# Recurrence plus two-layer MLP on one core: GLA stages spread between MLP pieces, TensorE order pinned by hand

## The chip, the cores and the metric

The kernel runs on one core of a Trainium2 chip. The metric is the time of one execution in microseconds of device time, as the median of several executions. The span of a profile, from the first to the last instruction of the program, is 1.7 us shorter than the time of the same execution. The kernel is written in a framework whose scheduler, when the program is built, settles the order of every engine's instructions: unless told otherwise it may put a later instruction ahead of an earlier one when data dependencies permit and its own estimate says that this is useful. "Free" below means that, and "pinned" means that TensorE keeps the order in which the program was written.

In the lines of profiles PE is TensorE (PEld its weight loads), DVE is VectorE, ACT is ScalarE, POOL is GpSimd, SP is SyncE. L170 is line 170 of that run's kernel; in the changed kernel and its variants all matmuls go through one helper (L128 in the lines shown) and all transposes through another (L131), so that the tile's name tells them apart.

## The reference

A gated linear recurrence ("GLA") over 4 batches, 8 heads, 768 steps and head size 48, then a two-layer MLP with squared ReLU ("MoE" in the kernel, though there is no routing) over the 3072 tokens:

```python
for t in range(S):                               # S = 768, state is 48 x 48 per head
    state = alpha[:, :, t, :, None] * state + np.einsum('bhd,bhe->bhde', k[:, :, t], v[:, :, t])
    y[:, :, t] = np.einsum('bhd,bhde->bhe', q[:, :, t], state)
x = y.transpose(0, 2, 1, 3).reshape(3072, 384)
h = x @ w_in                                     # 384 -> 2048
g = np.maximum(h, 0.0) ** 2
return g @ w_out                                 # 2048 -> 384
```

## The kernel before

The tokens are cut into 24 chunks of 128. A chunk's GLA is a chain that passes between engines many times. The MoE works on groups of chunks: "MoE-1" makes `ph` (three accumulated matmuls for each of 16 slices of the hidden layer), "MoE-2" makes `po` (16 accumulated matmuls for a chunk).

```python
def gla_chunk(sc, tiles):
    nc.scalar.activation(L[:, :, 0:D], at, AF.Ln)
    nc.tensor.matmul(pm[:, 0:HD], lhsT=utri_b[:, 0, :], rhs=L[:, :, 0:D], ...)   # decay
    nc.scalar.activation(A, pm..., AF.Exp); nc.scalar.activation(Ainv, pm..., AF.Exp, scale=-1.0)
    nc.vector.tensor_mul(qA[:, :, 0:D], qt, A); nc.vector.tensor_mul(kI[:, :, 0:D], kt, Ainv)
    # 8 transposes of qA, kI on TensorE, then
    nc.vector.tensor_copy(qkT, pT)
    # 8 score matmuls, then
    nc.vector.tensor_mul(sm[:, hh], sc_ps[:, hh], utri_b...)                     # twice
    # py = q state ("inter") + sm v ("intra"), then
    nc.scalar.copy(xn, py[:, 0:HD])
    # 3 transposes of xn, then
    nc.vector.tensor_copy(xT_big[:, :, tok0:tok0 + P], pxT)
    # state update: 4 matmuls, st * ae on VectorE, sb copy on ScalarE
    ...

def moe1(g, f):
    ph = ps_h.tile([P, 512], FP32, name="ph")            # 2 buffers
    # 3 matmuls of GN[g] * 128 columns
    nc.scalar.activation(r[:, 0:n], ph[:, 0:n], AF.Relu)
    eng = nc.vector if f % 2 == 0 else nc.gpsimd
    eng.tensor_mul(gT_tiles[g][:, f, 0:n], r[:, 0:n], r[:, 0:n])

def moe2(g, tt):
    po = ps_o.tile([P, d_model], FP32, name="po")        # 1 buffer
    # 16 matmuls of 384 columns, ob = copy of po by VectorE or ScalarE, DMA out

GN = [2, 2, 4, 4, 4, 4, 2, 2]                            # chunks per MoE group
# moe_q: for each group its 16 moe1 pieces, the moe2 tiles of the group before merged in
for s in range(NT):
    ...                                                  # loads for s + 2; w_out piece for s < 4
    gla_chunk(s, pend.pop(s))
    budget = total * max(0, s - 2) / (NT - 2)
    while qi < len(moe_q) and moe_q[qi][0] <= s and spent < budget:
        ...                                              # place the next MoE piece
```

A piece can be placed only when its whole group has been through GLA, and one chunk more (`moe_q[qi][0] <= s`; chunks count from 0), and the budget grows evenly from chunk 2 on. Counting the pieces that this loop places gives, after chunks 8, 12, 16 and 20, a whole 4-chunk group at once (16 MoE-1 pieces and 2 to 4 MoE-2 tiles), and nothing after the chunks between.

## Time and profile before

| | before |
|---|---|
| time, median of 3 (237.67 to 237.98) | 237.79 us |
| span of the profile | 235.9 us |
| PE busy by the page | 194.6 us (82%) |
| TensorE's need at undisturbed spacing | 162 us (MoE 124.5, GLA 37.9) |
| DVE / ACT busy | 55% / 55% |

The third row misleads. The Trainium skill ("Perfetto Trace Analysis", Identifying the Most-Contended Engine) says that matmul busy time is a poor measure of the distance to the limit, because matmuls are pipelined. The number used here instead is the *gap*: the time from one matmul's start to the next one's start, less the spacing of such matmuls when nothing disturbs them (read from the timeline: 215.5 ns for 512 columns, 162 for 384, 109 for 256, 55.5 for 128, 42.5 for 96, 25 for 48 or 1, 28 for a 64-row score matmul). The sums of spacings and gaps below were worked out so from the trace.

The page of before: its first line of busy times, three rows of the 40 slices of 5.9 us each (tenths of busy time; PEclk is the granted clock), and the chain of work that ended last, by engine:

```profile
PE 194.6 (82%) x1696; PEld 110.0 (47%) x1696; DVE 129.2 (55%) x253; ACT 129.4 (55%) x313; POOL 68.1 (29%) x101
...
PE   0055877887989979999989899998979979999974
...
PEclk9999999999999999999999999999999999999999
DMA  7999899931999965669747664245410000011001
...
PE 57%; ACT 15%; DVE 14%; issue 6%; DMA 3%; POOL 2%; SPq 1%; ACTq 0%; DVEq 0%; POOLq 0%
```

Until 48 us (slice 8) the DMA engines are full: inputs and weights are landing. After that TensorE is never long idle and never quite full.

The waits of TensorE in before, the longest two from 0 to 50 us and then four from 50 to 192 us (total us, times, longest):

```profile
PE misc L170 <- DVE qA_s L165: 9.1, 4, 7.0
PE misc L144 <- ACT L_s L141: 4.5, 2, 4.0
...
PE misc L170 <- DVE qA_s L165: 3.5, 6, 0.6
PE sc L180 <- DVE qkT L174: 3.1, 8, 0.6
PE misc L196 <- DVE sm L184: 2.5, 7, 0.5
PE misc L203 <- ACT xn L200: 1.5, 3, 0.6
```

Each of the last four is a step of the GLA chain that waits for the step before it on another engine. Why nothing else filled these holes shows in the timeline of TensorE, 112.5 to 117 us (start, duration, operation):

```profile
112.49 1.51 PE L226 MATMUL ph<-xT_big,w_in_b 128*128 128x512 bf16 x6
113.84 0.33 PE L239 MATMUL po<-w_out_b,gT_1095 128*128 128x384 bf16 x1
114.00 1.55 PE L226 MATMUL ph<-xT_big,w_in_b 128*128 128x512 bf16 x6
115.39 0.33 PE L144 MATMUL misc<-L_s,utri_b 128*128 128x384 bf16 x1
115.62 1.49 PE L226 MATMUL ph<-xT_big,w_in_b 128*128 128x512 bf16 x6
```

Here MoE-1 runs in a burst with almost no GLA between, as the placing loop wrote it. In the stretches between bursts, GLA chains have little but MoE-2 to fill their waits: from 120 to 132 us and from 156 to 168 us the trace has not one MoE-1 matmul.

### The profile page before, as it was taken

The page shows a single profiled execution, that of the slowest core. Times are in us where ns is not written, and L with a number is a line of the kernel's source. Part 1 is how long each engine was busy: PE and PEld are TensorE (multiplying, and loading weights), DVE is VectorE, ACT ScalarE, POOL GpSimd, SP SyncE. Part 2 cuts the span into 40 slices and gives each one's busy share as a digit, 9 for nine tenths or more (in the row PEclk, how much of TensorE's full clock was granted, in tenths as well). Part 3 has the DMA queues.
Part 4 walks back from the last instruction along what each step waited for, and adds up shares of the span by engine and source line. Part 5 has one row for each costly group of instructions (what it writes and reads, how often), then busy time and mean ns, then how long its engine had stood idle before and what let it go on. Part 6 is the DMA issues. An engine that isn't in the chain of part 4 may idle for free.

```text
span 235.9 us, 4581 instructions
## 1 busy us (share of the span) xinstructions
PE 194.6 (82%) x1696; PEld 110.0 (47%) x1696; DVE 129.2 (55%) x253; ACT 129.4 (55%) x313; POOL 68.1 (29%) x101
## 2 busy tenths in 40 slices
PE   0055877887989979999989899998979979999974
PEld 0033555554544435544444554455534436655642
DVE  0257567667567376567376557375655477135320
ACT  3234777695348765538854457835467727351720
POOL 4000333442002750005630006620016623320520
PEclk9999999999999999999999999999999999999999
DMA  7999899931999965669747664245410000011001
GB/s 138 311 249 269 218 257 259 248 61 35 209 216 214 216 130 97 163 143 184 152 85 166 150 138 94 65 98 129 103 44 0 3 0 35 36 61 40 3 35 67
DMA packets 107031, 30.19 MB, mean 128 GB/s; under 512 B 100352, under 2 KB 105472, under 8 KB 107008
## 3 DMA queue, kind: packets, MB, share of 16 engines
q1 hardware_dynamic: 107008, 29.89, 54.5%
q8 instruction: 13, 0.21, 0.4%
q14 instruction: 10, 0.08, 0.1%
HBM read 25.17 MB, written 4.72 MB: 127 GB/s over the span
## 4 chain that ended last, share of the span: by engine, by line
PE 57%; ACT 15%; DVE 14%; issue 6%; DMA 3%; POOL 2%; SPq 1%; ACTq 0%; DVEq 0%; POOLq 0%
PE po L239 20%; PE ph L226 20%; ACT r L231 5%; DVE sm L184 4%; DVE qA_s L165 3%; ACT A L153 3%; PE sc L180 3%; PE misc L203 3%; PE misc L170 3%; DMA win_f<-in_moe_w_in_dram 3%; DVE qkT L174 3%; PE misc L172 2%; PE misc L196 2%; PE misc L144 2%; DVE ob L245 2%
## 5 line engine op out<-in xcount | busy, mean ns | idle before, releaser
L226 PE MATMUL ph<-xT_big,w_in_b 128*128 128x512 bf16 (+1 forms) x384 | 79.6, 328 | 1.5 <-ACT r L231 0.5
L231 ACT ACTIVATE r<-ph 128x256 bf16<-128x256 f32 (+1 forms) x128 | 61.5, 492 | 24.0 <-PE ph L226 16.6
L226 PEld LDWEIGHTS <-w_in_b 128*128 128x128 bf16 x384 | 35.5, 98 | 25.6 <-issue 8.1
L162 POOL CAST vb<-vt 128x384 bf16<-128x384 f32 x24 | 13.0, 542 | 77.0 <-DMA vt<-in_v_dram 31.4
L184 DVE TENSOR_TENSOR sm<-sc,utri_b 128x512 bf16<-128x512 f32 x48 | 30.9, 685 | 2.8 <-PE sc L180 2.4
L200 ACT CAST xn<-misc 128x384 bf16<-128x384 f32 x24 | 11.5, 479 | 25.6 <-PE misc L196 25.6
L165 DVE TENSOR_TENSOR qA_s<-qt,A 128x384 bf16<-128x384 f32 x24 | 15.8, 659 | 13.6 <-ACT A L153 13.6
L174 DVE COPY qkT<-misc 128x1024 bf16<-128x1024 bf16 x24 | 16.5, 689 | 9.9 <-PE misc L172 9.9
L170 PE MATMUL misc<-ident_bf,qA_s 128*128 128x128 bf16 x96 | 10.1, 232 | 12.9 <-DVE qA_s L165 12.6
L215 ACT CAST sb<-st 128x384 bf16<-128x384 f32 x20 | 9.6, 480 | 20.1 <-DVE st L213 19.8
L204 DVE COPY xT_big<-misc 128x384 bf16<-128x384 bf16 x24 | 8.6, 357 | 20.2 <-PE misc L203 19.9
L196 PE MATMUL misc<-vb,sm 128*128 128x48 bf16 x192 | 13.1, 188 | 7.0 <-DVE sm L184 7.0
L153 ACT ACTIVATE A<-misc 128x384 bf16<-128x384 f32 x24 | 11.8, 490 | 11.7 <-PE misc L147 11.7
L196 PEld LDWEIGHTS <-sm 128*128 128x128 bf16 x192 | 9.4, 97 | 16.6 <-DVE sm L184 15.4
L170 PEld LDWEIGHTS <-qA_s 128*128 128x128 bf16 x96 | 5.9, 101 | 21.2 <-DVE qA_s L165 14.0
L239 PE MATMUL po<-w_out_b,gT_1095 128*128 128x384 bf16 x64 | 13.8, 325 | 0.8 <-DVE ob L245 0.5
L239 PE MATMUL po<-w_out_b,gT_1538 128*128 128x384 bf16 x64 | 13.5, 325 | 0.5 <-DVE ob L245 0.2
L141 ACT ACTIVATE L_s<-at 128x384 bf16<-128x384 f32 x24 | 12.6, 523 | 2.4 <-DMA at<-in_alpha_dram 2.0
L180 PE MATMUL sc<-qkT 64*128 64x128 bf16 x192 | 10.0, 226 | 4.0 <-DVE qkT L174 4.0
L166 DVE TENSOR_TENSOR kI_s<-kt,Ainv 128x384 bf16<-128x384 f32 x24 | 13.2, 550 | 0.0
L247 ACT COPY ob<-po 128x384 f32<-128x384 f32 x12 | 5.7, 478 | 13.1 <-PE po L239 12.9
L239 PE MATMUL po<-w_out_b,gT_2031 128*128 128x384 bf16 x64 | 12.8, 325 | 0.1
(66 smaller groups left out, 290.2 us busy)
## 6 DMA issues: line engine op xcount, KB each, us to landing
at<-in_alpha_dram SPq DMA_DIRECT2D x24, 192.0 KB, 3.6
qt<-in_q_dram SPq DMA_DIRECT2D x24, 192.0 KB, 3.5
kt<-in_k_dram SPq DMA_DIRECT2D x24, 192.0 KB, 3.7
vt<-in_v_dram SPq DMA_DIRECT2D x24, 192.0 KB, 3.7
out_dram<-ob SPq DMA_DIRECT2D x24, 192.0 KB, 1.9
win_f<-in_moe_w_in_dram SPq DMA_DIRECT2D x4, 768.0 KB, 6.1
wout_f<-in_moe_w_out_dram SPq DMA_DIRECT2D x4, 768.0 KB, 5.6
```

What stands on the lines that cost most here:

```text
L153: nc.scalar.activation(A, pm[:, 0:HD].rearrange("p (h d) -> p h d", h=H), AF.Exp)
L162: nc.gpsimd.tensor_copy(vb, vt)
L165: nc.vector.tensor_mul(qA[:, :, 0:D], qt, A)
L166: nc.vector.tensor_mul(kI[:, :, 0:D], kt, Ainv)
L170: nc.tensor.transpose(pT[:, p, :], qA[:, 2 * p:2 * p + 2, :], ident_bf)
L174: nc.vector.tensor_copy(qkT, pT)
L180: nc.tensor.matmul(sc_ps[:, hh, p, :], lhsT=qkT[sl, NP + p, :], rhs=qkT[sl, p, :], start=True, stop=True)
L184: nc.vector.tensor_mul(sm[:, hh], sc_ps[:, hh], utri_b.to_broadcast([P, NP, P]))
L196: nc.tensor.matmul(py[:, h * D:(h + 1) * D], lhsT=sm[:, hh, p, :], rhs=vb[:, h, :], start=(c == 0 and h == 0), stop=True, skip_group_check ...
L226: nc.tensor.matmul(ph[:, 0:n], lhsT=w_in_b[:, j, f * P:(f + 1) * P], rhs=xT_big[:, j, t0:t0 + n], start=(j == 0), stop=(j == KT - 1),)
L231: nc.scalar.activation(r[:, 0:n], ph[:, 0:n], AF.Relu)
L239: nc.tensor.matmul(po, lhsT=gT[:, kf, tt * P:(tt + 1) * P], rhs=w_out_b[:, kf, :], start=(kf == 0), stop=(kf == FT - 1),)
```

## The change

Its intent: cut GLA into five stages and write them into the program with MoE pieces between, so that every copy on VectorE or ScalarE passes behind MoE matmuls; pin TensorE to exactly that order. Groups become 3 chunks; MoE-2 tiles are placed in quarters, alternating with MoE-1; inputs are loaded three chunks ahead instead of two; the next chunk's decay is issued before this chunk's `intra`; and the MoE of a group is spread evenly until the next group is complete. The diff holds smaller changes too: two pieces of `w_out` are now loaded before the inputs of chunk 3 (one in before), `intra` takes its heads in another order, and in the last group every second MoE-2 tile gets another PSUM buffer. The core of the diff (stage bodies are the old lines moved, cut here):

```diff
+    def mm(*a, **kw):
+        tc.keep_in_program_order(nc.tensor.matmul(*a, **kw))
+    def tr(*a):
+        tc.keep_in_program_order(nc.tensor.transpose(*a))
-    def gla_chunk(sc, tiles):
+    def st_decay(s): ...
+    def st_transpose(s): ...
+    def st_scores(s): ...        # scores, inter product and state update
+    def st_intra(s): ...
+    def st_xT(s): ...
-    def moe2(g, tt):
+    NQ = 4
+    def moe2(g, tt, qd):
+        for kf in range(qd * FT // NQ, (qd + 1) * FT // NQ): ...
-    GN = [2, 2, 4, 4, 4, 4, 2, 2]
+    GN = [1, 2, 3, 3, 3, 3, 3, 3, 3]
+    def budget(tau):
+        b = 0.0
+        for g in range(len(GN)):
+            lo, hi = ends[g], ends[g + 1]
+            b += seg_cost[g] * min(1.0, max(0.0, (tau - lo) / (hi - lo)))
+        return b
-        gla_chunk(s, pend.pop(s))
-        budget = total * max(0, s - 2) / (NT - 2)
+        seq = [lambda: st_transpose(s), lambda: st_scores(s),
+               lambda: st_decay(s + 1) if s + 1 < NT else None,
+               lambda: st_intra(s), lambda: st_xT(s)]
+        for k, f in enumerate(seq):
+            f()
+            if k == 4:
+                prog["x"] = s + 1
+            moe_until(budget(s + (k + 1) / 5))
```

More of the change, by code (lines that the diff above doesn't have):

```diff
@@ L94 @@
     nc.vector.memset(ae_s, 0.0)
-    xT = [big.tile([P, KT, P], BF16, name=f"xT{i}") for i in range(NT)] if False else None
     xT_big = big.tile([P, KT, n_tok], BF16)
@@ L125, in load_chunk, with st_decay @@
             tiles.append(t)
-        return tiles
-    state = {}
-    def gla_chunk(sc, tiles):
-        b, c = divmod(sc, NCH)
-        at, qt, kt, vt = tiles
-        tok0 = sc * P
-        i = sc % NBUF
-        if c == 0:
-            state["ps"] = ps_st.tile([P, NP, 2 * D], FP32, name="st")
-            state["b"] = None
-        st = state["ps"]
+        ch[sc] = {"in": tiles}
+    def mm(*a, **kw):
+        tc.keep_in_program_order(nc.tensor.matmul(*a, **kw))
+    def tr(*a):
+        tc.keep_in_program_order(nc.tensor.transpose(*a))
+    ch = {}
+    state = {}
+    def st_decay(s):
+        d = ch[s]
+        at, qt, kt, vt = d["in"]
+        i = s % NBUF
         L = L_s[:, i]
         nc.scalar.activation(L[:, :, 0:D], at, AF.Ln)
+        vb = work.tile([P, H, D], BF16, name="vb", bufs=3)
+        nc.gpsimd.tensor_copy(vb, vt)
+        d["vb"] = vb
         pm = ps_misc.tile([P, 512], FP32, name="misc")
-        nc.tensor.matmul(pm[:, 0:HD], lhsT=utri_b[:, 0, :], rhs=L[:, :, 0:D],
-                         start=True, stop=True)
+        mm(pm[:, 0:HD], lhsT=utri_b[:, 0, :], rhs=L[:, :, 0:D], start=True, stop=True)
         for p in range(NP):
-            nc.tensor.matmul(
-                pm[:, HD + p:HD + p + 1],
-                lhsT=L[:, 2 * p:2 * p + 2, :], rhs=ones_col,
-                start=True, stop=True,
-            )
+            mm(pm[:, HD + p:HD + p + 1], lhsT=L[:, 2 * p:2 * p + 2, :], rhs=ones_col,
+               start=True, stop=True)
+        pm3 = pm[:, 0:HD].rearrange("p (h d) -> p h d", h=H)
         A = work.tile([P, H, D], BF16, name="A")
-        nc.scalar.activation(A, pm[:, 0:HD].rearrange("p (h d) -> p h d", h=H), AF.Exp)
+        nc.scalar.activation(A, pm3, AF.Exp)
         Ainv = work.tile([P, H, D], BF16, name="Ainv")
-        nc.scalar.activation(Ainv, pm[:, 0:HD].rearrange("p (h d) -> p h d", h=H),
-                             AF.Exp, scale=-1.0)
+        nc.scalar.activation(Ainv, pm3, AF.Exp, scale=-1.0)
         ae = ae_s[:, i]
@@ L159, in gla_chunk, with st_transpose, st_scores @@
         nc.scalar.activation(ae[64:128, :, 1], pm[64:128, HD:HD + NP], AF.Exp)
-        vb = work.tile([P, H, D], BF16, name="vb")
-        nc.gpsimd.tensor_copy(vb, vt)
-        qA = qA_s[:, i]
-        kI = kI_s[:, i]
-        nc.vector.tensor_mul(qA[:, :, 0:D], qt, A)
-        nc.vector.tensor_mul(kI[:, :, 0:D], kt, Ainv)
+        nc.vector.tensor_mul(qA_s[:, i, :, 0:D], qt, A)
+        nc.vector.tensor_mul(kI_s[:, i, :, 0:D], kt, Ainv)
+    def st_transpose(s):
+        d = ch[s]
+        i = s % NBUF
+        qA, kI = qA_s[:, i], kI_s[:, i]
         pT = ps_misc.tile([P, 2 * NP, P], BF16, name="misc")
         for p in range(NP):
-            nc.tensor.transpose(pT[:, p, :], qA[:, 2 * p:2 * p + 2, :], ident_bf)
+            tr(pT[:, p, :], qA[:, 2 * p:2 * p + 2, :], ident_bf)
         for p in range(NP):
-            nc.tensor.transpose(pT[:, NP + p, :], kI[:, 2 * p:2 * p + 2, :], ident_bf)
+            tr(pT[:, NP + p, :], kI[:, 2 * p:2 * p + 2, :], ident_bf)
         qkT = work.tile([P, 2 * NP, P], BF16, name="qkT")
         nc.vector.tensor_copy(qkT, pT)
+        d["qkT"] = qkT
+    def st_scores(s):
+        d = ch[s]
+        b, c = divmod(s, NCH)
+        i = s % NBUF
+        qkT = d["qkT"]
         sc_ps = ps_sc.tile([P, 2, NP, P], FP32, name="sc")
@@ L179, in gla_chunk @@
                 sl = slice(64 * hh, 64 * hh + 64)
-                nc.tensor.matmul(sc_ps[:, hh, p, :], lhsT=qkT[sl, NP + p, :],
-                                 rhs=qkT[sl, p, :], start=True, stop=True)
+                mm(sc_ps[:, hh, p, :], lhsT=qkT[sl, NP + p, :], rhs=qkT[sl, p, :],
+                   start=True, stop=True)
         sm = work.tile([P, 2, NP, P], BF16, name="sm")
         for hh in range(2):
-            nc.vector.tensor_mul(sm[:, hh], sc_ps[:, hh],
-                                 utri_b.to_broadcast([P, NP, P]))
+            nc.vector.tensor_mul(sm[:, hh], sc_ps[:, hh], utri_b.to_broadcast([P, NP, P]))
@@ L187, in gla_chunk @@
+        d["sm"] = sm
         py = ps_misc.tile([P, 512], FP32, name="misc")
-        for p in range(NP):
-            if c > 0:
-                nc.tensor.matmul(py[:, 2 * p * D:2 * (p + 1) * D], lhsT=qkT[:, p, :],
-                                 rhs=state["b"][:, p, :], start=(p == 0), stop=False,
-                                 skip_group_check=True)
-        for p in range(NP):
-            for hh in range(2):
-                h = 2 * p + hh
-                nc.tensor.matmul(py[:, h * D:(h + 1) * D], lhsT=sm[:, hh, p, :],
-                                 rhs=vb[:, h, :], start=(c == 0 and h == 0), stop=True,
-                                 skip_group_check=True)
@@ L199, in gla_chunk @@
-        xn = work.tile([P, HD], BF16, name="xn")
-        nc.scalar.copy(xn, py[:, 0:HD])
-        pxT = ps_misc.tile([P, KT, P], BF16, name="misc")
-        for j in range(KT):
-            nc.tensor.transpose(pxT[:, j, :], xn[:, j * P:(j + 1) * P], ident_bf)
-        nc.vector.tensor_copy(xT_big[:, :, tok0:tok0 + P], pxT)
+        d["py"] = py
+        if c > 0:
+            for p in range(NP):
+                mm(py[:, 2 * p * D:2 * (p + 1) * D], lhsT=qkT[:, p, :],
+                   rhs=state["b"][:, p, :], start=(p == 0), stop=False,
+                   skip_group_check=True)
@@ L206, in gla_chunk @@
         if c < NCH - 1:
+            if c == 0:
+                state["ps"] = ps_st.tile([P, NP, 2 * D], FP32, name="st")
+            st = state["ps"]
             for p in range(NP):
-                nc.tensor.matmul(st[:, p, :], lhsT=kI[:, 2 * p:2 * p + 2, :],
-                                 rhs=vb[:, 2 * p:2 * p + 2, :],
-                                 start=(c == 0 and p == 0), stop=True,
-                                 skip_group_check=True)
+                mm(st[:, p, :], lhsT=kI_s[:, i, 2 * p:2 * p + 2, :],
+                   rhs=d["vb"][:, 2 * p:2 * p + 2, :],
+                   start=(c == 0 and p == 0), stop=True, skip_group_check=True)
@@ L212, in gla_chunk @@
             st4 = st.rearrange("p n (j e) -> p n j e", j=2)
-            nc.vector.tensor_mul(st4, st4, bcast(ae, D))
+            nc.vector.tensor_mul(st4, st4, bcast(ae_s[:, i], D))
             sb = work.tile([P, NP, 2 * D], BF16, name="sb")
@@ L216, in gla_chunk, with st_intra, st_xT @@
             state["b"] = sb
+    def st_intra(s):
+        d = ch[s]
+        c = s % NCH
+        py, sm, vb = d["py"], d["sm"], d["vb"]
+        for hh in range(2):
+            for p in range(NP):
+                h = 2 * p + hh
+                mm(py[:, h * D:(h + 1) * D], lhsT=sm[:, hh, p, :], rhs=vb[:, h, :],
+                   start=(c == 0 and h == 0), stop=True, skip_group_check=True)
+        xn = work.tile([P, HD], BF16, name="xn")
+        nc.scalar.copy(xn, py[:, 0:HD])
+        d["xn"] = xn
+    def st_xT(s):
+        xn = ch[s]["xn"]
+        pxT = ps_misc.tile([P, KT, P], BF16, name="misc")
+        for j in range(KT):
+            tr(pxT[:, j, :], xn[:, j * P:(j + 1) * P], ident_bf)
+        nc.vector.tensor_copy(xT_big[:, :, s * P:(s + 1) * P], pxT)
+        del ch[s]
     gT_tiles = {}
+    po_cur = {}
     def moe1(g, f):
@@ L225, in moe1 @@
         for j in range(KT):
-            nc.tensor.matmul(
-                ph[:, 0:n], lhsT=w_in_b[:, j, f * P:(f + 1) * P],
-                rhs=xT_big[:, j, t0:t0 + n], start=(j == 0), stop=(j == KT - 1),
-            )
+            mm(ph[:, 0:n], lhsT=w_in_b[:, j, f * P:(f + 1) * P],
+               rhs=xT_big[:, j, t0:t0 + n], start=(j == 0), stop=(j == KT - 1))
         r = rpool.tile([P, 512], BF16, name="r")
@@ L233, in moe1 @@
         eng.tensor_mul(gT_tiles[g][:, f, 0:n], r[:, 0:n], r[:, 0:n])
-    def moe2(g, tt):
-        po = ps_o.tile([P, d_model], FP32, name="po")
-        gT = gT_tiles[g]
-        for kf in range(FT):
-            nc.tensor.matmul(
-                po, lhsT=gT[:, kf, tt * P:(tt + 1) * P], rhs=w_out_b[:, kf, :],
-                start=(kf == 0), stop=(kf == FT - 1),
-            )
-        ob = opool.tile([P, d_model], FP32, name="ob")
-        if tt % 2 == 0:
-            nc.vector.tensor_copy(ob, po)
-        else:
-            nc.scalar.copy(ob, po)
-        nc.sync.dma_start(out=out_r[GT[g] + tt], in_=ob)
@@ L250 @@
-    GN = [2, 2, 4, 4, 4, 4, 2, 2]
+    NQ = 4
+    def moe2(g, tt, qd):
+        if qd == 0:
+            last = g == len(GN) - 1
+            if last and tt % 2 == 1:
+                po_cur[0] = ps_misc.tile([P, 512], FP32, name="misc")[:, 0:d_model]
+            else:
+                po_cur[0] = ps_o.tile([P, d_model], FP32, name="po")
+        po = po_cur[0]
+        gT = gT_tiles[g]
+        for kf in range(qd * FT // NQ, (qd + 1) * FT // NQ):
+            mm(po, lhsT=gT[:, kf, tt * P:(tt + 1) * P], rhs=w_out_b[:, kf, :],
+               start=(kf == 0), stop=(kf == FT - 1))
+        if qd == NQ - 1:
+            ob = opool.tile([P, d_model], FP32, name="ob")
+            if tt % 2 == 0:
+                nc.vector.tensor_copy(ob, po)
+            else:
+                nc.scalar.copy(ob, po)
+            nc.sync.dma_start(out=out_r[GT[g] + tt], in_=ob)
@@ L251 @@
+    GN = [1, 2, 3, 3, 3, 3, 3, 3, 3]
     assert sum(GN) == NT
     GT = [sum(GN[:i]) for i in range(len(GN))]
-    LEAD = 2
-    pend = {}
-    for s in range(2):
-        pend[s] = load_chunk(s)
-        if s == 0:
-            for pc in range(2):
-                load_w_in(pc, 4)
-        else:
-            for pc in range(2, 4):
-                load_w_in(pc, 4)
-    moe_q = []
-    for g in range(len(GN)):
-        done = GT[g] + GN[g]
-        items = []
-        for f in range(FT):
-            items.append((done, "1", g, f))
-        if g > 0:
-            tts = GN[g - 1]
-            step = FT // tts
-            merged = []
-            for f in range(FT):
-                merged.append(items[f])
-                if (f + 1) % step == 0:
-                    merged.append((done, "2", g - 1, (f + 1) // step - 1))
-            items = merged
-        moe_q += items
@@ L281 @@
-    for tt in range(GN[-1]):
-        moe_q.append((NT, "2", len(GN) - 1, tt))
-    def cost(it):
-        return GN[it[2]] * 3 * P if it[1] == "1" else FT * d_model
-    total = sum(cost(it) for it in moe_q)
-    qi = 0
-    spent = 0
-    for s in range(NT):
-        if s + 2 < NT:
-            pend[s + 2] = load_chunk(s + 2)
-        if s < 4:
-            load_w_out(s, 4)
-        gla_chunk(s, pend.pop(s))
-        budget = total * max(0, s - 2) / (NT - 2)
-        while qi < len(moe_q) and moe_q[qi][0] <= s and spent < budget:
-            it = moe_q[qi]
-            (moe1 if it[1] == "1" else moe2)(it[2], it[3])
-            spent += cost(it)
-            qi += 1
@@ L302 @@
-    while qi < len(moe_q):
-        it = moe_q[qi]
-        (moe1 if it[1] == "1" else moe2)(it[2], it[3])
-        qi += 1
+    segs = []
+    for g in range(len(GN) + 1):
+        ones = [("1", g, f) for f in range(FT)] if g < len(GN) else []
+        twos = [("2", g - 1, tt, qd) for tt in range(GN[g - 1]) for qd in range(NQ)] if g else []
+        n1, n2 = len(ones), len(twos)
+        i1 = i2 = 0
+        seg = []
+        while i1 < n1 or i2 < n2:
+            if i1 < n1 and (i2 >= n2 or i1 * n2 <= i2 * n1):
+                seg.append(ones[i1])
+                i1 += 1
+            else:
+                seg.append(twos[i2])
+                i2 += 1
+        segs.append(seg)
@@ new lines, with cost @@
+    items = sum(segs, [])
+    def cost(it):
+        return GN[it[1]] * 3 * P if it[0] == "1" else FT * d_model // NQ
+    total = sum(cost(it) for it in items)
+    seg_cost = [sum(cost(it) for it in seg) for seg in segs]
+    ends = [GT[g] + GN[g] for g in range(len(GN))] + [NT + 1]
+    def budget(tau):
[4 more added lines that the diff above has]
+        return b
+    prog = {"i": 0, "spent": 0, "x": 0}
@@ new lines, in moe_until @@
+    def moe_until(budget):
+        while prog["i"] < len(items) and prog["spent"] < budget:
+            it = items[prog["i"]]
+            if it[0] == "1" and GT[it[1]] + GN[it[1]] > prog["x"]:
+                return
+            if it[0] == "1":
+                moe1(*it[1:])
+            else:
+                moe2(*it[1:])
+            prog["spent"] += cost(it)
+            prog["i"] += 1
+    for s in range(2):
+        load_chunk(s)
+        for pc in range(2 * s, 2 * s + 2):
+            load_w_in(pc, 4)
@@ new lines @@
+    load_chunk(2)
+    load_w_out(0, 4)
+    load_w_out(1, 4)
+    st_decay(0)
+    for s in range(NT):
+        if s + 3 < NT:
+            load_chunk(s + 3)
+        if s < 2:
+            load_w_out(s + 2, 4)
+        seq = [lambda: st_transpose(s), lambda: st_scores(s),
[6 more added lines that the diff above has]
+            moe_until(budget(s + (k + 1) / 5))
@@ L309 @@
+    moe_until(total + 1)
 _INS = ['q', 'k', 'v', 'alpha', 'moe_w_in', 'moe_w_out']
```

## The prediction

> **What bounds the kernel now.** TensorE, but through its order rather than its work. The page shows PE 82% busy, yet that counts pipelined ends. In the timeline, undisturbed matmuls start 162 ns apart for 384 columns, 215 for 512, 109 for 256, 55 for a 128-column transpose. The Trainium skill ("TensorE: Matmul & The Clock Gate", Part 1) gives N / 2.4 GHz + 2.5 ns; 384 columns make 162.5, so the trace agrees. Summed over all matmuls (my estimate from these spacings) MoE needs 124.5 us and GLA 37.9 us: 162 us of a 236 us span. The granted clock is full throughout.
>
> Where the other 74 us are: up to 24 us PE does only 3 us of work, because inputs and weights are still landing (DMA about 250 GB/s and saturated until 48 us, page part 2). From 24 to 48 us PE does 15 us. From 48 to 228 us it loses about 39 us: the wait view names qA_s, qkT, sm, xn (VectorE and ScalarE results that the next GLA step needs) and the copy of the single po buffer; in the timeline MoE-1 runs in bursts without GLA (72-84, 108-120, 144-156, 180-190 us), then GLA chunks follow each other with only MoE-2 to fill, and each waits for its own chain. GLA steps also cost 0.1-0.13 us at each entry (scores, state product) even without a wait.
>
> **What the change does.** It adds and removes almost no work. The same products are made; the middle groups go from 512 to 384 columns (same cycles per token), so ScalarE's relu has 128 instances again, about 0.49 us each (the 384-column evictions of before) instead of 0.38/0.60: +4 us on an engine that is 55% busy. It moves: MoE is paced so that about 1 us of it stands between any two dependent GLA steps, and next chunk's decay is issued two steps early. Latencies to cover: qkT copy 0.69 us, sm 1.37, xn 0.48, A/Ainv then qA/kI about 2 us. One fifth of a chunk's MoE is 5.2/5 = 1.04 us, so scores and intra are just covered when VectorE is free, and not when a gT product (0.4), st (0.56) or ob (0.55) stands ahead; ScalarE and VectorE take their queues in order. po stays single: each of 24 tiles still waits 0.2-0.6 us beyond the one MoE-1 piece set between.
>
> **Sum.** Start: still DMA bound; six chunks and all weights by about 49 us, PE work done 20 us against 18 before: gain about 1 us. The rest, 143 us, cost 39 us of gaps before. Now (estimate): entries 0.4 us a chunk, 7; po 6; GLA waits 0.6 us a chunk, 10; together about 23 us. The last 23 us are pure MoE at nearly full rate. 49 + 143 + 23 + 3 (last copy and store) = 218; with luck in the queues 208. All of it lies on the critical path, as PE is the path. I predict **216 us**, range **206 to 229**; faster by over 2%: 0.86, within: 0.10, slower: 0.04.
>
> **Would show it right:** PE's work in 12 us windows rises from 8-10 us to 10.5 or more after 60 us, evenly, no MoE-1 bursts; PE share of the chain of waits rises above 65%; waits of PE on qA_s and qkT shrink; the first 48 us unchanged; GLA's last chunk ends about 190 us instead of 217. **Wrong:** PE waiting in order for sm, qkT or ob in every chunk, VectorE over 75% busy in the middle.
>
> **What would spoil it:** fixed order makes any late VectorE or ScalarE result stop all of TensorE, where before ready work was placed there; a chunk that waits for DMA in the first 48 us stops MoE too; the pacing leaves 23 us of MoE after the last chunk, and little MoE in the first 40 us.

## More of the kernel before

In the first 40 us some gap is only the half clock. (The clock row of the page does not show all of that: before 24 us it reads full in before, while 128-column transposes start 107 ns apart.)

## The result, and the profile after

| | before | after |
|---|---|---|
| time, median of 4 | 237.73 us | 225.14 us (224.74 to 227.79) |
| span of the profile | 235.9 us | 223.2 us |
| TensorE's need | 162.4 us | 162.5 us |
| of it done by 50 us | 19.1 us | 15.7 us |
| gaps from 50 to 192 us | 30.9 us | 20.1 us |
| gaps after 192 us | 8.2 us | 2.1 us |
| start of the last chunk's xT copy | 216.8 us | 194.4 us |

The ratio is 0.9495, with a 95% interval of 0.9421 to 0.9569: faster by 5%. Every ratio in this document is the mean time of one kernel's fast runs over that of the other's of the same rounds, so it is not quite the ratio of the medians that are quoted.

The page after:

```profile
PE 184.1 (83%) x1744; PEld 117.6 (53%) x1744; DVE 129.9 (58%) x265; ACT 125.4 (56%) x325; POOL 70.9 (32%) x109
...
PE   1057659668998898999889989999989999999994
...
PEclk9999656999999999999999999999999999999999
DMA  6999999999895384989689853543100010010011
...
PE 50%; ACT 27%; DVE 10%; issue 7%; DMA 3%; SPq 1%; ACTq 0%; DVEq 0%
```

The middle is even now, but the fifth to ninth slices together hold less TensorE work than in before, and the granted clock sinks to about half in the fifth to seventh. The last line is the chain that ended last, by engine: PE holds 50% of it (57% before), and ACT 27% (15% before).

Waits of TensorE after, from 0 to 50 us:

```profile
PE misc L128 <- ACT L_s L141: 11.3, 5, 4.3
PE misc L131 <- DVE qA_s L158: 7.1, 1, 7.1
PE ph L128 <- ACT r L243: 2.4, 3, 1.1
```

And from 50 to 192 us:

```profile
PE misc L131 <- ACT xn L220: 4.8, 8, 1.1
PE ph L128 <- ACT r L243: 2.5, 11, 0.2
PE po L128 <- DVE ob L264: 2.0, 5, 0.5
PE ph L128 <- DVE xT_big L228: 0.8, 3, 0.3
PE sc L128 <- DVE qkT L171: 0.3, 1, 0.3
```

In the middle the waits for `qA_s`, `qkT` and `sm` are all but gone (9.1 us in before, 0.3 now), while those for `xn` grew from 1.5 to 4.8 us. In the start, the wait for `L_s` is new in size: 11.3 us against 4.5 us in before. `L_s` is the first ScalarE step of a chunk, the logarithm, and needs that chunk's `alpha` to have landed. The trace shows what it holds up: between 30.4 and 33.0 us TensorE stands still for `L_s` of chunk 3, and right after it come MoE-1 pieces, `intra` and x transposes of earlier chunks. The `alpha` itself came later: those of chunks 3, 4 and 5 landed at 31.8, 38.5 and 44.9 us, against 27.6, 34.5 and 40.7 us in before. The new place of the `w_out` loads ahead of chunk 3 fits that, but no run puts them back. It is not enough for the long wait by itself: in free_groups4 below, with landings at 31.9, 38.2 and 44.8 us, the wait for `L_s` is 6.0 us.

### The profile page after: what moved, and what is told of

The parts are those of the page before. It is cut to its first block, busy times and chain, and to the rows that moved or that the text cites. A ratio compares the mean times of both kernels' runs of the same rounds, so it can differ in the third digit from the quotient of the medians.

```text
span 223.2 us, 4722 instructions
## 1 busy us (share of the span) xinstructions
PE 184.1 (83%) x1744; PEld 117.6 (53%) x1744; DVE 129.9 (58%) x265; ACT 125.4 (56%) x325; POOL 70.9 (32%) x109
## 4 chain that ended last, share of the span: by engine, by line
PE 50%; ACT 27%; DVE 10%; issue 7%; DMA 3%; SPq 1%; ACTq 0%; DVEq 0%
PE po L128 19%; PE ph L128 14%; ACT r L243 8%; PE misc L128 6%; PE misc L131 6%; ACT A L152 4%; PE sc L128 4%; ACT Ainv L154 4%; ACT xn L220 3%; DVE qkT L171 3%; DMA win_f<-in_moe_w_in_dram 3%; DVE ob L264 3%; ACT L_s L141 2%; ACT sb L207 2%; PE st L128 2%
## 5 line engine op out<-in xcount | busy, mean ns | idle before, releaser
L243 ACT ACTIVATE r<-ph 128x384 bf16<-128x384 f32 (+2 forms) x144 | 64.3, 458 | 59.5 <-PE ph L128 55.6
L128 PE MATMUL ph<-xT_big,w_in_b 128*128 128x384 bf16 (+2 forms) x432 | 85.9, 318 | 6.2 <-ACT r L243 5.0
L128 PEld LDWEIGHTS <-w_in_b 128*128 128x128 bf16 x432 | 38.2, 102 | 23.3 <-issue 6.9
L128 PE MATMUL misc<-L_s,utri_b 128*128 128x384 bf16 x24 | 8.3, 346 | 11.3 <-ACT L_s L141 11.3
L128 PEld LDWEIGHTS <-qkT 64*128 64x128 bf16 (+1 forms) x272 | 9.9, 99 | 12.2 <-DVE qkT L171 6.4
L264 DVE COPY ob<-po 128x384 f32<-128x384 f32 x16 | 8.8, 548 | 8.1 <-PE po L128 8.1
L131 PE MATMUL misc<-ident_bf,xn 128*128 128x128 bf16 x72 | 8.6, 232 | 5.7 <-ACT xn L220 5.5
L128 PEld LDWEIGHTS <-L_s 128*128 128x128 bf16 x96 | 6.1, 99 | 12.5 <-issue 10.0
L154 ACT ACTIVATE Ainv<-misc 128x384 bf16<-128x384 f32 x24 | 11.9, 496 | 0.0
L245 POOL TENSOR_TENSOR gT_2836<-r 128x384 bf16<-128x384 bf16 x8 | 6.6, 827 | 15.9 <-ACT r L243 15.9
```

Source lines behind the costliest of these rows:

```text
L128: tc.keep_in_program_order(nc.tensor.matmul(*a, **kw))
L131: tc.keep_in_program_order(nc.tensor.transpose(*a))
L154: nc.scalar.activation(Ainv, pm3, AF.Exp, scale=-1.0)
L264: nc.vector.tensor_copy(ob, po)
```

## The experiments

The first theory (A) was the change's own: the hand-made order on TensorE brings the gain. The rival (B): the gain comes from what was rewritten in the program, and pinning it adds nothing. The second question was the start, which cost more than I had predicted. Twelve kernels ran, all correct.

| run | order | difference | time us | ratio to before |
|---|---|---|---|---|
| after | pinned | | 225.14 | 0.9495 |
| free_order | free | none else | 218.33 | 0.9182 |
| before_fixed | pinned | before's program | 338.26 | 1.4241 |
| whole_moe2 | pinned | whole MoE-2 tiles | 236.48 | 0.9942 |
| free_whole | free | whole MoE-2 tiles | 220.02 | 0.9246 |
| groups_of_4 | pinned | old groups | 222.05 | 0.9344 |
| free_groups4 | free | old groups | 211.34 | 0.8894 |
| start_late | pinned | decay late in first six chunks | 228.14 | 0.9587 |
| warm | pinned | extra matmuls in the start | 225.79 | 0.9494 |
| before_quarters | free | before + quarter tiles | 236.85 | 0.9951 |
| before_paced | free | before + even pacing | 224.37 | 0.9443 |
| free_block | free | MoE after each whole chunk | 216.95 | 0.9142 |
| best | free | groups 1,1,2,2,3,3,4,4,2,2 | 217.31 | 0.9154 |

### Is it the pinned order?

**free_order** takes the pinning away and leaves everything else.

```diff
     def mm(*a, **kw):
-        tc.keep_in_program_order(nc.tensor.matmul(*a, **kw))
+        nc.tensor.matmul(*a, **kw)
     def tr(*a):
-        tc.keep_in_program_order(nc.tensor.transpose(*a))
+        nc.tensor.transpose(*a)
```

> The changed kernel without the pinning of TensorE's order: stages, 3-chunk groups, quarter tiles and the program's order stay, but the scheduler may move matmuls as it did before. Theory A (the gain comes from the order fixed by hand on TensorE): about 232 to 238 us, gaps between matmuls from 48 us on back near 36 us, MoE-1 bursts again. Rival B (the gain comes from the new program order, pacing and pieces, which the scheduler would follow anyway): 223 to 227 us, as the changed kernel's 225.1.

It ran in 218.33 us (ratio 0.9182, 0.9156 to 0.9207). Both theories had missed the direction: pinned, the same program takes about 3% longer (0.9495 / 0.9182 = 1.034, each against before in its own rounds). Theory A falls. The scheduler did reorder: about half of TensorE's matmuls stand at another place in the list, and the lists of VectorE and ScalarE shift with it, so this is not a test of TensorE's order alone. Waits of TensorE in free_order, three from 0 to 50 us and one from 50 to 192 us:

```profile
PE misc L131 <- DVE qA_s L158: 8.3, 3, 6.8
PE misc L128 <- ACT L_s L141: 4.2, 1, 4.2
PE misc L128 <- DVE sm L187: 2.2, 6, 0.6
...
PE misc L131 <- ACT xn L220: 1.3, 3, 0.9
```

The wait for `L_s` is back at before's size. By 50 us TensorE has done 17.8 us of its work (15.7 pinned). In the middle the wait for `xn` is 1.3 us (4.8 pinned).

**before_fixed** is the kernel before with all matmuls and transposes through `mm` and `tr`, pinned.

> The kernel before with nothing but TensorE pinned to program order. Its program has a whole GLA chunk without MoE in it, then the MoE pieces. Theory A says that the order is what matters, so an unspread order must be bad when pinned: each chunk's chain (about 6 us in the first chunks of before, of which TensorE works 1.6 us) stands open, 24 times about 4 us: 290 us or more. Rival B (pinning itself helps): at or under 238 us.

338.26 us. The expectation of a far longer time holds; it says only that a program whose GLA chunk is one block relies on the scheduler for its overlap. The mean granted clock was 0.798, so the halts also cost clock.

**whole_moe2** and **free_whole** set `NQ = 1` in the place of `NQ = 4`, pinned and free.

> The changed kernel with whole MoE-2 tiles (16 matmuls, 2.6 us) in place of quarters. Theory A (even spreading covers the copies between GLA steps): a 2.6 us piece falls into one gap and leaves others with too little, and ScalarE and VectorE get MoE-1 results in bursts: 2 to 6 us longer, 227 to 231 us, with PE waits on r, qkT and xn up. Rival (quarters do not matter): within 1 us of the changed kernel.

> The free order with whole MoE-2 tiles. Theory Q (pieces small enough to fill one gap matter in any order): 222 to 230 us, well above the free order's 218.3. Rival (quarters matter only because a pinned order cannot move a piece to another gap; a scheduler can split 16 matmuls itself): 217 to 220 us.

Pinned, whole tiles cost 11 us (236.48 us), more than I had expected; free they cost under 2 us (220.02 us). So the quarters matter mostly because the order is pinned. The reading that a fixed order needs a piece of the right size in each hole, and that whole tiles leave other holes with MoE-1 alone, fits the waits below; a part of the 11 us lies in the start, where only 13.2 us of work were done by 50 us (15.7 in the changed kernel). Waits of TensorE in whole_moe2 from 50 to 192 us; that for `r` was 2.5 us in the changed kernel, and `sm` was not listed:

```profile
PE ph L128 <- ACT r L243: 6.4, 16, 1.0
PE misc L128 <- DVE sm L187: 3.1, 11, 0.4
```

**groups_of_4** and **free_groups4** put `GN = [2, 2, 4, 4, 4, 4, 2, 2]` back, pinned and free.

> The changed kernel with the old groups 2,2,4,4,4,4,2,2. Theory: TensorE work per token is the same, ScalarE saves 16 instances (about 4 us off its path), the first MoE starts a chunk later, at the end 15.6 us of pure MoE stay rather than 23.4, so GLA is less dense: within 2 us of the changed kernel. Rival (3-chunk groups are a main part of the gain): 229 us or more.

> The free order with groups 2,2,4,4,4,4,2,2. In the pinned order these groups were 3 us faster than 3-chunk groups. If that comes from the shorter pure-MoE end (17 us against 25) and fewer ScalarE instances, it holds here too: 214 to 217 us. If the scheduler had already hidden it: 217 to 220 us.

222.05 and 211.34 us. The 3-chunk groups are no part of the gain: in both orders they lose, 3 us pinned and 7 us free. Both expectations were too timid. free_groups4 is the fastest kernel, 11% under before. Its row of TensorE (slices of 5.2 us), and the longest of its waits of TensorE from 50 to 192 us:

```profile
PE   1056499689999999999999999999999999999993
...
PE misc L131 <- ACT xn L220: 2.5, 9, 0.4
PE ph L128 <- ACT r L243: 0.7, 3, 0.3
PE sc L128 <- DVE qkT L171: 0.3, 1, 0.3
```

TensorE did 20.0 us of work by 50 us and lost 13.5 us in gaps from 50 to 192 us (17.8 and 19.3 in free_order). One reading is that a 512-column piece takes TensorE 0.65 us and ScalarE 0.60 us to evict, a 384-column piece 0.49 us and 0.49 us, so wider pieces leave ScalarE and the single `po` buffer more time. The shorter wait for `r` (0.7 against 2.4 us) fits, but no run isolates it. The clock differs as well: from 24 to 48 us it was 1.00 in free_groups4 and 0.79 in free_order.

### Then what is the gain?

**before_quarters** adds only quarter tiles, spread between MoE-1 pieces, to the kernel before.

```diff
-        for kf in range(FT):
+        for kf in range(qd * FT // NQ, (qd + 1) * FT // NQ):
...
-            tts = GN[g - 1]
+            tts = GN[g - 1] * NQ
```

> The kernel before with only this: MoE-2 tiles in quarters, spread evenly between MoE-1 pieces of the next group. GLA stays one block per chunk and the scheduler stays free. If the quarters alternating with MoE-1 are a part of the gain by themselves (bursts of MoE-1 end, ScalarE is spread): 228 to 234 us. If the gain needs the GLA stages spread in the program: 235 to 240 us.

236.85 us; the interval of its ratio (0.9897 to 1.0006) includes no change. The quarters by themselves are nothing. My expectation then concluded that the GLA stages have to be spread. The next two runs refuted that conclusion.

**before_paced** changes only how many MoE pieces are placed after a chunk, and from when on they may be placed. GLA stays one block.

```diff
-    total = sum(cost(it) for it in moe_q)
+    # segs[g]: cost of group g's moe1 and group g-1's moe2; ends[g]: chunks done when g is complete
+    def paced(tau):
+        return sum(segs[g] * min(1.0, max(0.0, (tau - ends[g]) / (ends[g + 1] - ends[g])))
+                   for g in range(len(GN)))
...
-        budget = total * max(0, s - 2) / (NT - 2)
-        while qi < len(moe_q) and moe_q[qi][0] <= s and spent < budget:
+        budget = paced(s + 1)
+        while qi < len(moe_q) and moe_q[qi][0] <= s + 1 and spent < budget:
```

> The kernel before, scheduler free, GLA one block per chunk, whole MoE-2 tiles, old groups; only the pacing is the changed kernel's: the MoE of a group is spread over the chunks until the next group is complete, where before a budget that ran ahead of what was ready put a whole group's MoE-1 into one burst. Theory P (pacing is the main part of the gain): 220 to 228 us, no MoE-1 bursts without GLA, waits on qA_s and qkT down. Rival G (the gain needs the GLA stages cut and the decay issued early): 232 to 238 us.

224.37 us (ratio 0.9443, 0.9406 to 0.9481). This edit of one loop gives what the whole change gives, net (0.9495, intervals overlap). It does two things, the even budget and leave to start a group one chunk sooner; which of them counts was not tested. TensorE's timeline in the time where before had a burst, and then three waits of TensorE from 50 to 192 us:

```profile
113.53 0.33 PE L239 MATMUL po<-w_out_b,gT 128*128 128x384 bf16 x1
113.77 0.40 PE L172 MATMUL misc<-ident_bf,kI_s 128*128 128x128 bf16 x4
114.00 0.33 PE L208 MATMUL st<-vb,kI_s 128*128 128x96 bf16 x4
114.17 0.65 PE L239 MATMUL po<-w_out_b,gT 128*128 128x384 bf16 x3
114.66 0.38 PE L226 MATMUL ph<-xT_big,w_in_b 128*128 128x512 bf16 x1
114.97 0.40 PE L180 MATMUL sc<-qkT 64*128 64x128 bf16 x8
115.30 0.34 PE L190 MATMUL misc<-sb,qkT 128*128 128x96 bf16 x4
115.48 1.03 PE L226 MATMUL ph<-xT_big,w_in_b 128*128 128x512 bf16 x4
...
PE misc L170 <- DVE qA_s L165: 2.4, 6, 0.6
PE sc L180 <- DVE qkT L174: 1.2, 4, 0.3
PE misc L196 <- DVE sm L184: 1.0, 3, 0.4
```

GLA steps and both kinds of MoE alternate, though the program has the chunk as one block: the scheduler spread them. Work done by 50 us is 19.4 us, as in before (19.1); gaps from 50 to 192 us are 21.7 us (30.9), and after that 3.7 us (8.2). The gain is all after the start.

**free_block** is free_order with all of a chunk's MoE placed after its five stages.

```diff
-            moe_until(budget(s + (k + 1) / 5))
+            if k == 4:
+                moe_until(budget(s + 1))
```

> The free order with all MoE of a chunk placed after its five GLA stages in the program; early decay, quarters, groups and pacing stay. Theory P (pacing does it, and the scheduler finds the places inside a chunk by itself): 217 to 222 us. Rival G (the program's spreading inside a chunk is needed even when the scheduler is free): 226 us or more. Pinned to program order such a program had cost far more (before_fixed, 338 us).

216.95 us (ratio 0.9142, 0.9095 to 0.9188): no worse than with the stages spread (0.9182). When the scheduler is free, writing the stages between the pieces by hand buys nothing. free_block still beats before_paced by 7 us, although its 3-chunk groups cost 7 us (free_groups4). The cleaner pair is before_paced and free_groups4, both free, both paced and with the same groups: 224.37 and 211.34 us. So the rest of the rewrite is worth 13 us, as much again as the pacing. It was not taken apart. Quarters are under 2 us of it by free_whole and spreading the stages is nothing by free_block. The early decay is a candidate: gaps before the transposes of `qA` and `kI` after 50 us are 6.3 us in before_paced and 0.4 us in free_groups4.

### Where was the start lost?

**start_late** tests whether the early decay, stopping on a chunk that has not landed, is the cost of pinning in the start.

```diff
+        if s < 6:
+            seq = seq[:2] + seq[3:] + seq[2:3]     # transpose, scores, intra, xT, decay
...                                                    # the chunk's end is marked after xT
```

> The changed kernel, order still pinned, but for the first six chunks the next chunk's decay stands after the transposes of x rather than before the intra products. Theory S (pinning costs about 7 us against the free order because, while inputs still land, the decay of a chunk that has not arrived stops MoE, intra and x transposes that are ready behind it): the 7.9 us of gaps before decay in the first 50 us shrink to under 4, and the time falls 3 to 5 us to 220 to 222. Rival (the free order's gain lies in the steady part): within 1.5 us of 225.1.

228.14 us: worse by 3 us instead of better. Waits of TensorE from 0 to 50 us:

```profile
PE misc L131 <- DVE qA_s L158: 10.4, 5, 6.7
PE misc L128 <- ACT L_s L141: 5.8, 3, 4.0
PE misc L131 <- ACT xn L220: 2.5, 4, 0.9
```

The wait for `L_s` did fall from 11.3 to 5.8 us, but those for `qA_s` and `xn` rose from 7.1 to 10.4 and from 0.7 to 2.5 us: the late decay has its own chain behind it. In a pinned order the hole moved; it did not close. The theory named a true wait, and its removal was not worth what I had said.

**warm** puts useless matmuls (512 columns, on a constant tile `junk`) after each stage of the first four chunks, so that TensorE stays busy.

```diff
             moe_until(budget(s + (k + 1) / 5))
+            if s < 4:
+                warm = ps_h.tile([P, 512], FP32, name="ph")
+                for _ in range(6 if k == 1 else 2):
+                    mm(warm, lhsT=ident_bf, rhs=junk, start=True, stop=True)
```

> The changed kernel with extra matmuls of no use put before the waits of the first four chunks, to keep TensorE busy enough for the full clock (the changed kernel has 0.51 granted in 24 to 36 us and 107 ns between 128-column transposes until 36 us; before only until 26 us). Theory C (the half clock costs time): full clock by 28 us and 2 to 4 us off, 221 to 223 us. Rival (TensorE waits for data there anyway): 224 to 228 us although the clock is full.

The window from 24 to 36 us, first in after, then in warm (window, its length, busy time and count of PE, PEld, DVE, ACT and POOL, granted clock, DMA share, GB/s):

```profile
24.00:36.00 12.00, 7.90 (x88) 6.47 (x86) 6.58 (x17) 8.24 (x25) 2.48 (x7) 0.51 0.98 261
```

```profile
24.00:36.00 12.00, 9.30 (x108) 5.89 (x106) 7.24 (x18) 8.09 (x25) 2.90 (x7) 1.00 0.96 262
```

The clock went from 0.51 to 1.00 and the time did not move (225.79 us, ratio 0.9494 against 0.9495). The half clock in the start looks like a symptom and not a cost: the DMA engines are 96 to 98% busy there, and the decay of chunks 3, 4 and 5 starts at 32.7, 40.6 and 47.6 us in warm against 33.0, 40.6 and 48.0 us in after. What the run does not exclude is that the 56 added matmuls, 12 us of TensorE's time in a pinned order, ate a small gain.

**best** tried to give TensorE more to do early, with free order and `GN = [1, 1, 2, 2, 3, 3, 4, 4, 2, 2]`.

> The free order with groups 1,1,2,2,3,3,4,4,2,2: more MoE is ready in the first 50 us, where TensorE did only 18 us of work, and the end is short. If TensorE can fill the start while inputs land: work done at 50 us 20 us or more, time 211 to 215 us. If the start is bound by the landing inputs and by ScalarE and VectorE (small groups mean more instances): no better than free_groups4.

217.31 us, 6 us above free_groups4, and work done by 50 us only 16.9 us. One-chunk groups are a bad start: I had reckoned with more ready work and got less. 128-column MoE-1 costs ScalarE 0.28 us for a piece and 512-column 0.60 us, so the relu of a token costs nearly twice as much. Gaps before MoE-1 in the first 50 us are 9.5 us (3.0 in free_groups4), some of it half clock. That the relu is the reason is argued, not isolated.

## Why the prediction was right or wrong

The time lies in the range (225.14 in 206 to 229), and faster by over 2% came true. The gain was 12.6 us rather than the 21.8 us I had named. I had credited the order by hand and the pacing together; the pacing was confirmed, the order was not.

- **The middle: right in size.** I expected 23 us of gaps after 49 us. Measured are 20.1 us from 50 to 192 us and 2.1 us after that, 22.2 together. The make-up was different: the entries of `scores` and `inter` 4.7 us (I had said 7), gaps before MoE-2 4.5 us (6 for `po`), x transposes 6.0 us, and MoE-1, which I had not counted, 6.4 us. TensorE's work in 12 us windows from 60 to 192 us is even (9.8 to 10.9 us, 8.0 to 11.0 in before), but reaches the 10.5 us that I had named in only five of eleven.
- **The start: the mis-sized term.** "Six chunks and all weights by about 49 us, PE work done 20 us" and "gain about 1 us". The landing came as said: all weights by 44.2 us and six chunks by 47.7 us. The work did not: measured are 15.7 us by 50 us, which is 3.4 us less than before had done. I had named the cause among the spoilers ("a chunk that waits for DMA in the first 48 us stops MoE too") and put no number on it. In numbers: 50 us + (162.5 - 15.7) us of work + 22.2 us of gaps + 3.6 us from the last matmul's start to the end make 222.6 us, against a span of 223.2.
- **The sum.** My 218 was a sum of spans; 1.7 us from the span to the timed figure were left out. I then went down to 216 for luck. There was none.
- **"All of it lies on the critical path, as PE is the path": wrong.** I said that PE's share of the chain would rise above 65%; it fell from 57% to 50%, and ScalarE's rose to 27%. The pinned order is not the reason: free_order has 47%, and it is faster. The share of the chain does not follow the time here.
- **"The first 48 us unchanged": wrong**, as above. **"GLA's last chunk ends about 190 us": close**, 194.4 us. **Waits on `qA_s` and `qkT` shrink: right**, those on `xn` grew instead. **VectorE over 75% busy in the middle**, named as a sign of being wrong: 18.4 of 24 us (77%) from 48 to 72 us, at most 67% in the 24 us windows after that, and no long wait of TensorE for VectorE in either.
- **What the prediction credited.** It read the bursts of MoE-1 in before rightly as the fault, and took the pacing, the stages spread by hand and the pinned order together for the cure. It did name among the spoilers that a fixed order lets any late result stop all of TensorE, and put no number on that either. The pacing of the placing loop alone gives as much as the whole change (before_paced). The runs give a path from one kernel to the other, by their medians: pacing -13.1 us (before to before_paced), the rest of the rewrite -13.0 (to free_groups4), 3-chunk groups +7.0 (to free_order), pinning +6.8 (to after). On another path the steps would have other sizes; pinning with the old groups costs 10.7 us. That the time fell in my range is therefore in part luck: 26 us of gain and 14 us of loss along this path, and I had put a number on neither. The pinned order costs: in all four programs that were run both ways, the free one was faster, by 3% (after), 5% (old groups), 7% (whole tiles) and 30% (before's program).

Open: how the 13 us between before_paced and free_groups4 share out; whether the change without its pacing would keep any of its gain, which no run shows; why wide groups are better in the middle; whether the place of the `w_out` loads costs time in the start; and whether another hand-made order would beat the scheduler's. That this one does not is shown; that none does is not.

## What to carry to other kernels

When a scheduler orders the engines, first look at what the program hands it in each stretch: work that is written in bursts stays in bursts, and spreading it evenly was here worth as much as the whole change, and half of the best kernel's gain. Pin an order only after the same program has run unpinned, and be most careful where data is still landing, since there one late input stops everything written after it. A half clock in a stretch that waits for DMA was here no visible cost; ask what TensorE waits for before you warm it.

## What the Trainium skill lacked or had wrong

- "TensorE: Matmul & The Clock Gate", Part 1, gives N / 2.4 GHz + 2.5 ns between warm matmuls, and the traces agree (162 ns for 384 columns, 215 for 512). The same page, Back-to-back issue gap, gives about 131 ns for 512 columns and 81 ns for 128 in a stream with a weight load for each matmul. These runs show a median of 215 ns over 192 such matmuls of 512 columns and 56 ns for 128-column transposes, each with its own weight load.
- The same page, Part 4, says that the full clock does not engage for transposes. Here the spacing of the program's 128-column transposes follows the granted clock: in the changed kernel 107 ns from 26 to 28 us at 0.50, and 56 ns from 50 us on at 1.00. The trace does not show whether the transpose mode was on in them.
- The same page, Part 1, says that one busy window of some 3.4 us releases the full clock, but not how busy it must be. In the changed kernel the clock stayed near half (0.51) from 24 to 36 us with TensorE at 66% by the page; with 78% and the extra matmuls of 512 columns (warm) it was full.
- "TensorEngine Tiling (Array Packing)", Key Properties, names a drain when the tiling mode changes, but no page has the price of a switch between 64-row and 128-row matmuls. The `inter` product that followed the 64-row scores started 148 ns after the last score in 16 of 16 cases in before, from 48 us on, with no wait shown; the next pair of scores starts 53 ns after the one before, so this is 95 ns late. Scores after a 384-column matmul start at best 258 ns after it, where 162 is usual: 96 ns late.
- "Perfetto Trace Analysis", Optimization Strategy, advises to interleave regimes with different limits. before_paced supports it (0.9443), but the page does not say that a pinned order can lose what interleaving wins (1.034 here).
